# The second expert's list due three f-tiles later, its first rows turned by TensorE, and a search's first counts handed over later

## The chip, the cores and the metric

The kernel runs on one core of a Trainium2 chip. The metric is the device time of one execution in microseconds (us), as the median of several runs. One of the runs of the kernel before was recorded by the hardware profiler; every row below comes from that one execution.

## The reference

An attention without softmax feeds a mixture of experts. The second part is the one that the change touches:

```python
scores = scale * np.matmul(z, z.transpose(0, 2, 1))      # 8 batches of 2496 rows, width 256
attn = np.maximum(scores, 0.0) ** 2
x = (u * np.matmul(attn, v)).reshape(19968, 256)
logits = x @ w_gate                                       # 8 experts
for idx in np.argsort(-logits.flatten()):                 # best pair first, everywhere
    tok, e = idx // 8, idx % 8
    if assigned[tok] >= 0 or counts[e] >= 2496: continue  # an expert takes 2496 rows and is full
    assigned[tok] = e; counts[e] += 1
for e in range(8):
    h = np.maximum(x[assigned == e] @ w1[e], 0.0)         # 256 -> 1024
    out[assigned == e] = h @ w2[e]                        # 1024 -> 256
```

## The kernel before

The attention fills the span up to about 1430 us. The experts follow, one after another, in the order in which they fill up, and the order in which they fill is found while the one before is being computed.

**The work of an expert.** Its 2496 rows are five groups (four of 512 rows, the last of 448). A group takes eight f-tiles, one for each 128 of the 1024 hidden columns. For each f-tile TensorE (PE) computes the first layer into a PSUM tile `hp` (`expand_part`, L672 to L674, three matmuls for each half of the 256 inputs, since every operand is held as a high and a low part). ScalarE (ACT) makes `hh` from it (L750), VectorE (DVE) makes the low part `hl_` (L752; in the group of 448 rows also the tail of `hh`, L755), and three f-tiles later PE does the second layer from both (`contract`, L765, L768, L770) into four accumulators y0 to y3.

**The rows of a group** are fetched by GpSimd (POOL) with four indirect DMAs (`gather_x`, L590), which need the expert's list `idx`. Then they must be turned. Nearly all groups use `tip_x`: DVE transposes blocks of 32 by 32 (L652), SyncE (SP) writes them to DRAM and reads them back in the wanted order (L655, L658), and `split_x` makes the high part on ACT (L665) and the low part on DVE (L666). Only the second group of the first expert uses `turn_x`: eight transposes on PE (L642) into the PSUM tile `xp` and one of the two `hp`, then ACT (L646) and DVE (L647).

Behind a group's last f-tile `put_y` adds the two parts of its rows (L793) and POOL scatters them to the output (L801).

**The route** of expert k (`route(k)`) finds its list, spread over the f-tiles of expert k-1. It closes the expert that is full (L338), finds each row's best open expert (`best_expert`, L80 to L97), and makes sortable integer keys (`order_keys`, L100 to L118). Then it searches a threshold in two stages of six rounds: in a round DVE compares the keys with seven or three candidates (`at_least`, L124, tile `mask`), PE counts the hits (`hist`, L281, tile `srch`), DVE and PE reduce the counts (L286 to L415). From the threshold come the expert's number, the load of its weights and, by a matmul L478 and some matmuls over `ob` (L523, L529), the list `idx` (L534). The weights are split by ACT (L618) and DVE (L621).

**The order.** The main loop writes the program in one fixed order per engine, a step per f-tile: `layer2` of f-tile n, what is due at n, a piece of the route, `layer1` of f-tile n + 3, another piece of the route. The dues are given by `at(n, ...)`: n0 is the first f-tile of a group, and gathers are due at n0 - 12, transposes at n0 - 8, splits at n0 - 4; the second expert's first group (1, 0) has the gather at n0 - 10 and the transpose at n0 - 7. The route's pieces are paced by `advance`: each `yield w` counts w steps, a window of half positions has 88 steps (`YIELDS`), and whatever is left when the window ends is handed over at once. The steps of a route add up to more than 88, so each window ends with such a rest, whose last instructions are the list's; the next route begins right behind it. The windows of the routes 1 and 2 meet at 2 * (PER + LATE), with PER = 40 f-tiles of an expert and LATE = 2.

"Turnover" below is the stretch of a route's end and the next one's start: from the matmul L478 to the first counts L281 of the next route, some 51 us. There are six of them, and a seventh end without a search behind it.

Of the kernel before, what the change touches and what calls it, by code (L numbers as in the profile page):

```python
# [135 lines left out]
def moe(tc, xd, first, jp, identf, w1, w2, out, B, S, cp, dram):  # L136
# [19 lines left out]
    ND = 15  # L156
    LA = 3
    AHEAD = 12
    LATE = 2
    YIELDS = 88  # L160
    with ExitStack() as ctx:
        rp = ctx.enter_context(tc.tile_pool(name="rp", bufs=1))
# [169 lines left out]
        def route(k):  # L332
            if k:
                closed = rp.tile([128, E], F32, name="closed", tag="rab")
                nc.vector.tensor_scalar(closed, ROUTE[k - 1]["star"], SHUT, None, op0=OP.mult)
                for c in range(0, JP, JP // 2):
                    o = lg[:, c:c + JP // 2]
                    nc.vector.tensor_add(o, o, closed[:, None, :].to_broadcast([128, JP // 2, E]))  # L338
                    yield 0.7
                for c in range(0, JP, JP // 4):  # L340
                    eq = rp.tile([128, JP // 4, E], BF, name="eq")
                    best_expert(nc, first, slice(c, c + JP // 4), eq)
                    yield 6.8 / 4
                done = rp.tile([128, JP], F32, name="done")
                with behind(1):
                    nc.vector.tensor_scalar(done, asg, 0.0, GONE, op0=OP.is_gt, op1=OP.mult)
                nc.vector.tensor_add(m, m, done)
                order_keys(nc, first, slice(0, JP))
                yield 1.5
            last = k == E - 1  # L350

            def take():
# [4 lines left out]
            if last:  # L357
                g = rp.tile([128, 2, JP], BF, name="fmask")
                nc.vector.tensor_scalar(g[:, 1], m, -3.1e38, None, op0=OP.is_gt)
                take()  # L360
                full = rp.tile([128, E], F32, name="full")
                nc.vector.tensor_scalar(full, rem, FULL / 2, None, op0=OP.is_lt)
            else:
                with behind(1):
                    nrem = rp.tile([128, E], F32, name="nrem")
                    nc.vector.tensor_mul(nrem, rem, dN)
                    nrow = rp.tile([128, 1], F32, name="nrow")
                    nc.vector.tensor_reduce(nrow, nrem, axis=AX.X, op=OP.add)
                    nc.vector.tensor_copy(hd[:, :, 16], nrow.to_broadcast([128, ND]))
                widths, step, at0, next0 = plans[k > 0]  # L370
                for stage in range(2):
                    V = floor
                    for r, w in enumerate(widths):
                        n = (1 << w) - 1
                        if r == 0:
                            T = first["at0"] if k == stage == 0 else at0
                        else:
                            T = rp.tile([128, ND], I16, name="T", bufs=2)
                            nc.vector.tensor_tensor(T[:, :n], W[:, :n], Dg.to_broadcast([128, n]), op=OP.add)
                        mask = []  # L380
                        whole = first["mask0"] if n > 7 else rp.tile([128, JP, n], BF, name="mask")
                        cuts = [0, JP] if k else [JP - 16, JP] if T is first["at0"] else [0, JP // 2, JP]
                        for lo, hi in zip(cuts, cuts[1:]):
                            at_least(nc, whole, xr, T[:, :n], lo, hi)
                        mask.append((0, lambda j, t=whole, n=n: t[:, j, :n]))
                        yield 2
                        if k:
                            x, nn = hist(mask, n, "jt")
                        else:
                            p, o = quad_hist(mask[0][1], n, r)  # L390
                        warm(k, 4)
                        if r:
                            V2 = rp.tile([128, 1], F32, name="V", bufs=2)
                            nc.vector.tensor_tensor(V2, V, Dg, op=OP.add)
                            V = V2
                        if r == 0:
                            W = next0
                        elif r + 1 < len(widths):
                            W = rp.tile([128, ND], F32, name="W", bufs=2)
                            n2 = (1 << widths[r + 1]) - 1  # L400
                            nc.vector.tensor_tensor(W[:, :n2], step[:, r + 1, :n2], V.to_broadcast([128, n2]), op=OP.add)
                        yield 2.2
                        if k:
                            o = srch()[:, :E * nn]
                            nc.tensor.matmul(o, onesr, x[:, :, :nn], start=True, stop=True)
                        else:
                            quad_sums(p, o, n, "jt")
                        warm(k, 10 if r + 1 < len(widths) or stage else 30)
                        best = rp.tile([128, E, ND], F32, name="best")
                        nc.vector.scalar_tensor_tensor(best[:, :, :n],  # L410
                                                       o.rearrange("p (e t) -> p e t", e=E)[:, :, :n], 0.0,
                                                       step[:, r, None, :n].to_broadcast([128, E, n]),
                                                       op0=OP.is_ge, op1=OP.mult)
                        Dg = rp.tile([128, 1], F32, name="Dg", bufs=2)
                        nc.vector.tensor_reduce(Dg, best[:, :, :n], axis=AX.XY, op=OP.max)  # L415
                    tstar = rp.tile([128, 1], F32, name="tstar")
                    nc.vector.tensor_tensor(tstar, V, Dg, op=OP.add)
                    if stage == 0:
                        base = rp.tile([128, 1], F32, name="base")
                        nc.vector.tensor_scalar(base, tstar, 65536.0, None, op0=OP.mult)  # L420
                        rel = rp.tile([128, JP], F32, name="rel")
                        nc.vector.scalar_tensor_tensor(rel, first["top"], base, first["low"],
                                                       op0=OP.subtract, op1=OP.add)
                        near = rp.tile([128, JP], I16, name="near")
                        nc.vector.tensor_scalar(near, rel, 32767.0, -32768.0, op0=OP.min, op1=OP.max)
                        spread(nc, xr, near)
                        yield 1.5
                T = tstar
                g = rp.tile([128, 2, JP], BF, name="fmask")
                nc.vector.tensor_scalar(g[:, 0], rel, T, None, op0=OP.is_ge)  # L430
                nc.vector.tensor_scalar(g[:, 1], rel, T, None, op0=OP.is_gt)
                take()
                yield
                if k:
                    x, nn = hist([(0, lambda j: g[:, :, j])], 2, "tj")
                    yield
                    o = srch()[:, :E * 2]
                    nc.tensor.matmul(o, onesr, x[:, :, :2], start=True, stop=True)
                else:
                    p, o = quad_hist(lambda j: g[:, :, j], 2, 1)  # L440
                    warm(k, 4)
                    quad_sums(p, o, 2, "tj")
                warm(k, 20)
                o = o.rearrange("p (e t) -> p e t", t=2)
                full = rp.tile([128, E], F32, name="full")
                nc.vector.tensor_scalar(full, o[:, :, 0], 0.0, None, op0=OP.is_ge)
                nc.vector.tensor_scalar(rem, o[:, :, 1], -1.0, None, op0=OP.mult)
# [60 lines left out]
            if k:  # L508
                p = srch()
                for c in range(0, JP, CB):  # L510
# [16 lines left out]
                    for j in range(c, min(J, c + CB)):  # L527
                        n, r = divmod(j - c, QW)
# [283 lines left out]
        def at(n, f, *a):  # L812
            todo.setdefault(n, []).append((f, a))

        for k in range(E):
            for g in range(NG):
                n0 = (k * NG + g) * FT
                if n0:
                    at(1 if (k, g) == (0, 1) else n0 - AHEAD + (LATE if (k, g) == (1, 0) else 0), gather_x, k, g)
                    if (k, g) == (0, 1):  # L820
                        at(n0 - 4, turn_x, k, g, range(DH))
                    else:
                        at(n0 - (7 if (k, g) == (1, 0) else 8), tip_x, k, g)
                        at(n0 - 4, split_x, k, g)
                at(n0 + FT - 1, put_y, k, g)
            n0 = k * PER
# [482 lines left out]
```

## Time and profile before

| what | value |
|---|---|
| median of three runs | 2431.34 us (2430.28 to 2432.57) |
| the profiled execution's own time | 2432.56 us |
| its span | 2430.5 us |
| PE busy | 2380.0 us (98%) |
| DVE busy | 2068.5 us (85%) |
| ACT busy | 1521.4 us (63%) |
| POOL busy | 460.6 us (19%) |

Busy times are sums over the whole span, so an engine with 85% can still be the one that sets the pace in a part of it. The span is shorter than the execution's time by 2.06 us, which lie ahead of and behind the recorded instructions.

### The profile page before, as it was taken

What the parts mean: (1) busy time and instruction counts of PE and PEld (TensorE: products, weight loads), DVE (VectorE), ACT (ScalarE), POOL (GpSimd) and SP (SyncE); (2) the same over time, 40 slices, a digit from 0 to 9 for tenths busy, and PEclk for the clock granted to TensorE, in tenths of its full rate; (3) what the DMA queues carried; (4) which work ended last, traced back from release to release, by engine and by line L of the source; (5) the groups of instructions that cost most, each with busy time, mean ns of one, the idle gap of its engine ahead of it and who ended that gap; (6) DMA issues with size and microseconds to landing.
All of it is one profiled execution on the core that took longest, in us unless ns stands there. A gap on an engine that the chain in (4) does not pass through costs nothing.

```text
span 2430.5 us, 42677 instructions
## 1 busy us (share of the span) xinstructions
PE 2380.0 (98%) x14724; PEld 1983.2 (82%) x14724; DVE 2068.5 (85%) x6220; ACT 1521.4 (63%) x2890; POOL 460.6 (19%) x690
## 2 busy tenths in 40 slices
PE   8999999999999999999999999899999999999998
PEld 6888888888888888888887787787888888888887
DVE  7898998998999998989989798979797979797443
ACT  7888888888888988888888223333332333333332
POOL 3020020020010200200100022333233333333332
PEclk9999999999999999999999999999999999999999
DMA  5153261261251532611511023232323323243331
GB/s 154 43 148 86 57 160 43 58 176 53 71 145 44 138 95 57 159 43 53 137 53 43 10 66 118 78 109 80 115 87 95 111 84 118 78 124 119 98 96 57
DMA packets 233848, 222.28 MB, mean 91 GB/s; under 512 B 95392, under 2 KB 192672, under 8 KB 233504
## 3 DMA queue, kind: packets, MB, share of 16 engines
q1 hardware_dynamic: 193088, 150.58, 21.3%
q0 software_dynamic: 40544, 68.98, 10.5%
q8 instruction: 116, 1.90, 0.3%
q14 instruction: 100, 0.82, 0.1%
HBM read 158.67 MB, written 60.82 MB: 90 GB/s over the span
## 4 chain that ended last, share of the span: by engine, by line
PE 82%; DVE 10%; issue 4%; POOL 1%; ACT 1%; DMA 1%; POOLq 0%; DVEq 0%; SPq 0%; ACTq 0%
PE acc L1038 41%; PE sc L996 11%; PE y L768 8%; PE hp L672 4%; PE hp L674 4%; PE hp L673 4%; PE y L770 4%; PE srch L281 2%; PE acc L1043 1%; POOL xg L590 1%; DVE mask L124 1%; DVE ob L523 1%; DVE w1l L621 1%; PE xp L325 1%; PE srch L529 1%
## 5 line engine op out<-in xcount | busy, mean ns | idle before, releaser
L1025 DVE TENSOR_TENSOR lo<-r,hi 128x512 fp32r<-128x512 f32 (+1 forms) x800 | 536.1, 673 | 83.1 <-ACT hi L1017 80.1
L1038 PE MATMUL acc<-hi,vh 128*128 128x512 f32 (+1 forms) x1520 | 590.8, 389 | 0.2 <-ACT vh L970 0.2
L1038 PE MATMUL acc<-lo,vh 128*128 128x512 f32 (+1 forms) x1520 | 587.7, 387 | 2.7 <-DVE lo L1025 2.7
L1038 PE MATMUL acc<-hi,vl 128*128 128x512 f32 (+1 forms) x1520 | 585.9, 385 | 0.0
L750 ACT ACTIVATE hh<-hp 128x512 fp32r<-128x512 f32 (+1 forms) x319 | 187.3, 587 | 629.9 <-PE hp L674 518.4
L1017 ACT ACTIVATE hi<-r 128x512 fp32r<-128x512 f32 (+1 forms) x780 | 500.2, 641 | 122.1 <-ACT r L1012 87.0
L1012 ACT ACTIVATE r<-r 128x512 f32<-128x512 f32 (+1 forms) x800 | 503.6, 639 | 2.5 <-DVE r L1006 2.4
L1079 DVE SCALAR_TENSOR_TENSOR lt<-xs,wgb 128x256 bf16<-128x256 f32 x1192 | 449.2, 417 | 0.0
L768 PE MATMUL y<-w,hh 128*128 128x512 f32 x1216 | 444.8, 399 | 0.7 <-DVE y L793 0.7
L1038 PEld LDWEIGHTS acc<-hi,vh 128*128 128x128 f32 x1520 | 286.2, 188 | 67.0 <-issue 13.8
L1008 ACT ACTIVATE r<-sc 128x512 f32<-128x512 f32 (+1 forms) x638 | 312.4, 614 | 40.3 <-PE sc L996 39.7
L1038 PEld LDWEIGHTS acc<-lo,vh 128*128 128x128 f32 x1520 | 286.3, 188 | 59.2 <-DVE lo L1025 8.2
L1038 PEld LDWEIGHTS acc<-hi,vl 128*128 128x128 f32 x1520 | 286.3, 188 | 52.1
L590 POOL DMA_INDIRECT xg<-xd,idx x160 | 181.2, 1133 | 513.3 <-DVE xg L628 281.1
L768 PEld LDWEIGHTS y<-w,hh 128*128 128x128 f32 x1216 | 229.0, 189 | 49.0 <-DVE y L793 2.2
L672 PE MATMUL hp<-xh,w1h 128*128 128x512 f32 (+2 forms) x642 | 256.5, 400 | 3.6 <-DVE hh L755 2.7
L673 PE MATMUL hp<-xl,w1h 128*128 128x512 f32 (+2 forms) x642 | 252.5, 393 | 1.2 <-DVE xl L666 1.1
L674 PE MATMUL hp<-xh,w1l 128*128 128x512 f32 (+2 forms) x642 | 250.6, 390 | 0.0
L996 PE MATMUL sc<-z,z 64*128 64x512 f32 (+1 forms) x1920 | 236.9, 389 | 4.2 <-ACT z L961 2.8
L996 PEld LDWEIGHTS sc<-z,z 64*128 64x128 f32 x1920 | 200.7, 185 | 31.2 <-ACT z L961 3.5
L959 POOL DMA_DIRECT2D z<-in_z_dram x35 | 18.7, 534 | 960.0 <-DVE lt L1079 530.0
L801 POOL DMA_INDIRECT out_dram<-y,idx x160 | 160.4, 1003 | 207.8 <-DVE y L793 120.9
(1193 smaller groups left out, 3152.1 us busy)
## 6 DMA issues: line engine op xcount, KB each, us to landing
ur<-in_u_dram SPq DMA_DIRECT2D x39, 512.0 KB
flat<-tr SPq DMA_DIRECT2D x152, 128.0 KB
xt<-flat SPq DMA_DIRECT2D x38, 512.0 KB
vh<-in_v_dram POOLq DMA_DIRECT2D x133, 128.0 KB
vr<-in_v_dram SPq DMA_DIRECT2D x32, 512.0 KB
xd<-tr SPq DMA_DIRECT2D x128, 128.0 KB
xs<-xd SPq DMA_DIRECT2D x32, 512.0 KB
wr<-in_moe_w_dram SPq DMA_DIRECT2D x32, 512.0 KB
```

The lines of the kernel that those rows point to most:

```text
L590: return nc.gpsimd.indirect_dma_start(out=dst, out_offset=None, in_=src, in_offset=bass.IndirectOffsetOnAxis(ap=idx, axis=0))
L672: nc.tensor.matmul(p[:, c], wh, xh, start=(d == 0), stop=False)
L673: nc.tensor.matmul(p[:, c], wh, xl, start=False, stop=False)
L674: latest["mm"] = nc.tensor.matmul(p[:, c], wl, xh, start=False, stop=(d == DH - 1))
L768: nc.tensor.matmul(o, h[:, c], w.rearrange("p s d -> p (s d)"), start=(f == 0), stop=(f == FT - 1), skip_group_check=True)
L996: nc.tensor.matmul(pair[s], key[b, p][r, c * 128:c * 128 + 128], query[b, g][r, :w], start=key is ZH and query is ZH, stop=key is ZL)
L1008: recent["r"] = nc.scalar.activation(r, p, AF.Relu, scale=scale)
L1012: nc.scalar.activation(R[n], R[n], AF.Square)
L1017: nc.scalar.activation(h, R[n], AF.Copy)
L1025: recent["l"] = nc.vector.tensor_sub(LO[n], a, h.bitcast(F32))
L1038: nc.tensor.matmul(o[d], w[:, c[d]], x, start=(kt == 0 and i == 0), stop=False)
L1079: nc.vector.scalar_tensor_tensor(t[r], src[r], 1.0, WG["rows"][r, e], op0=OP.mult, op1=OP.mult, accum_out=lg[r, j, e:e + 1])
```

## The change

It has four edits. `LATE` goes from 2 to 5: the windows of the routes 1 and 2 meet three f-tiles later, and the gather of group (1, 0) is due at n0 - 7. Group (1, 0) is turned by `turn_x` at n0 - 4, in place of `tip_x` at n0 - 7 and `split_x` at n0 - 4. Behind `order_keys` the step counts 3 and not 1.5. In the first round of a search a step of 1 is put between the instructions of the masks and the step of 2 that stands behind every round's masks, so that the counts are handed over later.

```diff
-    LATE = 2
+    LATE = 5
     YIELDS = 88
...
                 order_keys(nc, first, slice(0, JP))
-                yield 1.5
+                yield 3
...
                             at_least(nc, whole, xr, T[:, :n], lo, hi)
+                        if k and r == stage == 0:
+                            yield 1
                         mask.append((0, lambda j, t=whole, n=n: t[:, j, :n]))
                         yield 2
...
                     at(1 if (k, g) == (0, 1) else n0 - AHEAD + (LATE if (k, g) == (1, 0) else 0), gather_x, k, g)
-                    if (k, g) == (0, 1):
+                    if (k, g) in ((0, 1), (1, 0)):
                         at(n0 - 4, turn_x, k, g, range(DH))
                     else:
-                        at(n0 - (7 if (k, g) == (1, 0) else 8), tip_x, k, g)
+                        at(n0 - 8, tip_x, k, g)
                         at(n0 - 4, split_x, k, g)
```

Two lines are added, so that every line behind L385 has a number higher by two in the changed kernel: L281 stays, L672 becomes L674, L752 becomes L754, L768 and L770 become L770 and L772.

The program rows show what moves. First PE at the end of the turnover from route 3 to route 4 (the later ones are alike), before: the second layer of two f-tiles, then the counts.

```order
L768 MATMUL y_24342<-w_22683,hh 128x512
L770 MATMUL y_24342<-w_22683,hl__24329 128x256
L768 MATMUL y_24343<-w_22683,hh 128x512
L770 MATMUL y_24343<-w_22683,hl__24329 128x256
L768 MATMUL y_24344<-w_22683,hh 128x512
L770 MATMUL y_24344<-w_22683,hl__24329 128x256
L765 MATMUL y_24345<-w_22683,hh 128x512
L768 MATMUL y_24342<-w_22683,hh 128x512
L768 MATMUL y_24343<-w_22683,hh 128x512
L768 MATMUL y_24344<-w_22683,hh 128x512
L281 LDWEIGHTS oh
L281 MATMUL srch<-mask,oh 128x112
```

The same place in the changed kernel, the line numbers two higher but for L281:

```order
L770 MATMUL y_24345<-w_22684,hh 128x512
L772 MATMUL y_24343<-w_22684,hl__24374 128x256
L772 MATMUL y_24344<-w_22684,hl__24374 128x256
L674 MATMUL hp<-xh_24191,w1h 128x448
L675 MATMUL hp<-xl_24192,w1h 128x448
L676 MATMUL hp<-xh_24191,w1l 128x448
L674 MATMUL hp<-xh_24195,w1h 128x448
L675 MATMUL hp<-xl_24196,w1h 128x448
L676 MATMUL hp<-xh_24195,w1l 128x448
L772 MATMUL y_24345<-w_22684,hl__24374 128x256
L281 LDWEIGHTS oh
L281 MATMUL srch<-mask,oh 128x112
```

The second-layer matmuls on `hl__24374` and an f-tile's six first-layer matmuls now stand ahead of the counts. On DVE the same place before has the last keys, a piece of the weights' split, the masks, and behind them an f-tile's low part:

```order
L133 COPY rep<-key 128x640
L97 TENSOR_TENSOR oh<-code,code8b 128x320
L116 TENSOR_SCALAR top<-key 128x160
L118 CAST low<-key 128x160
L621 TENSOR_TENSOR w_22683<-wr,w_22683 128x2x256
L366 TENSOR_TENSOR nrem<-rem,dN 128x8
L124 TENSOR_TENSOR mask<-rep,at_17956 128x1120
L368 TENSOR_REDUCE nrow<-nrem 128x1
L752 SCALAR_TENSOR_TENSOR hl__22701<-hp,hh 128x384
```

In the changed kernel it reads:

```order
L133 COPY rep<-key 128x640
L97 TENSOR_TENSOR oh<-code,code8b 128x320
L116 TENSOR_SCALAR top<-key 128x160
L118 CAST low<-key 128x160
L623 TENSOR_TENSOR w_22684<-wr,w_22684 128x2x256
L754 SCALAR_TENSOR_TENSOR hl__22695<-hp,hh 128x384
L757 SCALAR_TENSOR_TENSOR hh<-hp,hh 128x64
L623 TENSOR_TENSOR w_22684<-wr,w_22684 128x2x256
L366 TENSOR_TENSOR nrem<-rem,dN 128x8
L124 TENSOR_TENSOR mask<-rep,at_17956 128x1120
```

An f-tile's low part and one more piece of the split have come between the keys and the masks; the keys still stand ahead of that low part. Last, PE at the first turnover of the changed kernel, where group (1, 0) is turned: the transposes come in pairs, one pair for each of the four gathers, between matmuls of the second layer.

```order
L644 MATMUL xp<-identf,xg 128x128
L644 MATMUL hp<-identf,xg 128x128
L767 MATMUL y_20798<-w_19465,hh 128x512
L644 MATMUL xp<-identf,xg 128x128
L644 MATMUL hp<-identf,xg 128x128
L770 MATMUL y_20795<-w_19465,hh 128x512
L644 MATMUL xp<-identf,xg 128x128
L644 MATMUL hp<-identf,xg 128x128
L770 MATMUL y_20796<-w_19465,hh 128x512
L770 MATMUL y_20797<-w_19465,hh 128x512
```

On DVE, where the list (`idx`, 18 instructions earlier) is made by the rest of route 1, the low parts of these rows stand among the instructions of `best_expert` of route 2:

```order
L80 TENSOR_REDUCE m<-lg 128x40
L95 TENSOR_TENSOR code<-eq 128x40
L80 TENSOR_REDUCE m<-lg 128x40
L97 TENSOR_TENSOR oh<-code,code8b 128x320
L82 TENSOR_TENSOR eq<-lg,m 128x320
L754 SCALAR_TENSOR_TENSOR hl__21056<-hp,hh 128x384
L84 TENSOR_TENSOR eq<-eq,code8b 128x320
L757 SCALAR_TENSOR_TENSOR hh<-hp,hh 128x64
L91 TENSOR_TENSOR eq<-eq 128x40x4
L649 TENSOR_TENSOR xl_21078<-xp,xh_21077 128x512
L93 TENSOR_TENSOR eq<-eq 128x40x2
L649 TENSOR_TENSOR xl_21082<-hp,xh_21081 128x512
```

Both L649 come 18 and 20 instructions behind the list, and the rest of the keys and the masks of route 2 stand behind them.

## Rows read from the trace of the kernel before

**Rows 1.** PE's waits by cause, 1540 to 2431: total us, times, longest.

```profile
PE srch L281 <- DVE mask L124: 9.8, 5, 3.3
```

**Rows 2.** Timeline of PE: start, us, instruction, idle before it and releaser.

```profile
1562.42 0.66 PE L281 MATMUL srch<-mask,oh 128*128 128x112 bf16 x10 [0.51 <-PE y L765]
...
1564.54 0.50 PE L673 MATMUL hp<-xl,w1h 128*128 128x512 f32 x1 [0.87 <-DVE xl L666]
...
1680.20 0.35 PE L281 MATMUL srch<-mask,oh 128*128 128x112 bf16 x2 [3.32 <-DVE mask L124]
...
2185.38 0.38 PE L770 MATMUL y<-w,hl__29448 128*128 128x256 f32 x1 [2.04 <-DVE hl__29448 L752]
```

**Rows 3.** Stretches: us, busy PE, PEld, DVE, ACT, POOL, PEclk, DMA, GB/s.

```profile
1509.05:1556.65 47.60, 42.17 (x336) 35.92 (x335) 47.39 (x116) 16.62 (x28) 12.69 (x12) 0.93 0.34 112
1547.28:1549.35 2.07, 2.07 (x12) 1.79 (x12) 2.07 (x8) 0.00 (x0) 1.46 (x3) 1.00 0.24 87
...
1629.22:1680.20 50.98, 47.66 (x377) 40.25 (x377) 50.08 (x117) 19.70 (x35) 18.51 (x16) 1.00 0.38 123
1680.20:1755.73 75.53, 75.52 (x471) 62.29 (x471) 58.81 (x190) 22.81 (x45) 24.26 (x24) 0.98 0.29 84
1755.73:1806.93 51.20, 49.08 (x383) 41.62 (x382) 50.58 (x118) 19.66 (x35) 19.34 (x16) 1.00 0.40 124
1806.93:1881.35 74.42, 74.29 (x471) 60.98 (x471) 58.72 (x190) 22.81 (x45) 24.29 (x24) 1.00 0.29 85
...
1680.20:1683.40 3.20, 3.20 (x18) 3.03 (x18) 3.20 (x11) 0.00 (x0) 0.00 (x0) 0.50 0.50 160
...
2058.25:2061.45 3.20, 3.20 (x19) 2.94 (x19) 3.20 (x11) 0.00 (x0) 0.00 (x0) 0.59 0.50 162
```

**Rows 4.** Timeline of DVE, the masks of route 4, then two rows of other places.

```profile
1805.40 0.67 DVE L621 TENSOR_TENSOR w<-wr,w 128x512 fp32r<-128x512 f32 x1
1806.00 0.15 DVE L366 TENSOR_TENSOR nrem<-rem,dN 128x8 f32<-128x8 f32 x1
1806.08 0.80 DVE L124 TENSOR_TENSOR mask<-rep,at 128x1120 bf16<-128x1120 int16 x1
...
1806.88 0.54 DVE L752 SCALAR_TENSOR_TENSOR hl__24380<-hp,hh 128x384 fp32r<-128x384 f32 x1
...
1442.57 0.68 DVE L752 SCALAR_TENSOR_TENSOR hl__19574<-hp,hh 128x512 fp32r<-128x512 f32 x1
...
1543.06 1.09 DVE L621 TENSOR_TENSOR w1l<-wr,w1h 128x512 fp32r<-128x512 f32 x1
```

**Rows 5.** Timeline of PE, matmuls back to back.

```profile
1801.30 0.28 PE L770 MATMUL y<-w,hl__24282 128*128 128x256 f32 x1
1801.42 0.39 PE L765 MATMUL y<-w,hh 128*128 128x512 f32 x1
1801.65 0.36 PE L672 MATMUL hp<-xh,w1h 128*128 128x448 f32 x1
1801.85 0.36 PE L673 MATMUL hp<-xl,w1h 128*128 128x448 f32 x1
```

**Rows 6.** Timelines of POOL and DVE: the gather and turning of group (1, 0).

```profile
1540.50 0.99 POOL L590 DMA_INDIRECT xg<-xd,idx  x1 [25.84 <-DVE idx L534]
...
1545.23 0.95 POOL L590 DMA_INDIRECT xg<-xd,idx  x1 [0.30 <-issue]
...
1549.58 1.24 DVE L652 STREAM_TRANSPOSE tr<-xg 128x1024 f32<-128x1024 f32 x1
```

**Rows 7.** Timelines of POOL, PE and ACT: group (0, 1), turned by PE.

```profile
1440.76 1.00 POOL L590 DMA_INDIRECT xg<-xd,idx  x1 [0.30 <-issue]
...
1443.66 0.33 PE L642 MATMUL xp<-identf,xg 128*128 128x128 f32 x1 [0.39 <-DMA xg<-xd,idx]
1443.83 0.60 PE L642 MATMUL hp<-identf,xg 128*128 128x128 f32 x4
...
1444.03 0.60 ACT L646 ACTIVATE xh<-xp 128x512 fp32r<-128x512 f32 x1 [1.86 <-PE xp L642]
```

## The prediction

> **What bounds the kernel now.** I read the table of busy times first, then PE's waits by cause, then the timeline at each wait, and last the stretches around them. PE is busy for 98% of the span, so there are few microseconds to win, and all of them in the experts' part lie where PE waits. The list of causes names one above all: five times the first counts of a search, L281, wait for DVE's masks, 9.8 us together, 3.3 us at most [rows 1]. The timeline shows the longest at 1680.20 and a wait of another kind, 2.04 us at the seventh turnover, where the second layer waits for DVE's low part [rows 2]. The reader is to see next, in the stretches, that a turnover is DVE's time and the rest of a period PE's: from 1755.73 to 1806.93 DVE is busy 50.58 of 51.20 us and PE 49.08, from 1806.93 to 1881.35 PE is busy 74.29 of 74.42 us and DVE 58.72 [rows 3]. The turnovers at 1509 and 1629 look alike: DVE 47.39 of 47.60 and 50.08 of 50.98 us [rows 3]. Two rules follow. In a turnover an instruction more on DVE makes the turnover longer by its whole time. And PE work that is moved from the turnover into the rest of the period costs its whole time too, since PE has no room there, while in the turnover it lay in PE's waits.
>
> **The later counts at the four last turnovers.** These are from route 3 on to the end of route 6. I counted in the program order what stands between L478 and the first counts (at the last one, the same stretch), before and now. PE has six matmuls of 448 columns more, seven of 512 columns in the first layer less, four of 512 in the second layer less (one for each of y0 to y3) and one of 256 less. Start to start they take 0.20, 0.23 and 0.12 us [rows 5], so 1.20 - 1.61 - 0.92 - 0.12 = -1.45 us of PE work. DVE has one L621 of the second weights more, 0.60 us from its start to the next one's [rows 4], and one low part of 512 columns is replaced by one of 384 and a short tail, which I set equal (0.68 against 0.54 us and the tail [rows 4]). So the turnover is longer by 0.60 us and holds 1.45 us less of PE's work: 2.05 us lost, PE's wait there growing from 51.20 - 49.08 = 2.12 [rows 3] to about 4.2 us. Four times this is 8.2 us. The masks are hidden by the f-tile that now stands ahead of the counts. What is late next is that f-tile's neighbour: the low part `hl__24374`, which the second layer needs, stands on DVE behind the keys and an L621, so the wait changes its name from L281 to L772. Behind the waiting L772 PE's queue holds the next six matmuls of the first layer, and the counts. If DVE has 0.60 us of slack that I don't see, a turnover costs 1.45; if the tail and the L621 run at their full 0.67 with a tail of some 0.1 to 0.2, it costs 2.3. I keep 5.8 to 9.2 for the four and take 8.2.
>
> **The later counts at the turnover from route 2 to route 3.** The same count gives six matmuls of 448 more, seven of 512 in the first layer less, eight of 512 and five of 256 in the second layer less: 1.20 - 1.61 - 1.84 - 0.60 = -2.85 us of PE work. DVE has one L621 more and one low part of 512 less, 0.60 against 0.68: nothing. I take +2.85, with 1.5 as the low end, if the pieces missing there include some that PE would have done in a wait anyway.
>
> **The second expert's first rows.** At the first turnover DVE gets two L621 of the first weights (1.09 each [rows 4]), one of the second (0.60), two L647 (no row of the size is shown; the nearest is the 128x512 of 0.68 [rows 4]) and loses two L652 of 1.24 [rows 6]; of the low parts two of 512 go and three of 384 come, 3 * 0.54 - 2 * 0.68 = 0.26. Sum: 2.18 + 0.60 + 1.36 - 2.48 + 0.26 = 1.9, and with the three tails 2.0. SP loses five DMAs, which nothing else waits for. On POOL the gather moves behind the scatters of group (0, 3); so far these stood behind it while POOL was idle for the list [rows 6], and only the buffer of y hangs on them, so I take nothing for it. The transposes add some 0.95 us to PE: eight, of which four are done in 0.60 us, 0.15 each at most [rows 7].
>
> Then there is a wait that was not there. The rows are fetched once the list is there: POOL stood 25.84 us idle for it [rows 6]. A gather takes 0.99 us and 0.30 to the next, so the fourth starts 3.87 after the first; in this place it was 4.73, since the third took longer [rows 6]. A gather lands 2.90 us after its start (1440.76 to 1443.66), ACT starts 0.37 later and takes 0.60 [rows 7]. So L647 can't start until 3.87 + 2.90 + 0.37 + 0.60 = 7.7 us (8.6 by the slower gathers) after the first gather. Between the list and L647 DVE has 18 short instructions; in a stretch of such ones eight take 2.07 us, seven of them whole [rows 3], so 18 take 4.7 to 5.3. DVE, which had been busy throughout, stands for 2.4 to 3.9 us at L647; I take 2.6, near the quicker gathers, as the longer one was a single case. Queued behind it are the rest of the keys and the masks of route 2, and for these PE's counts wait. PE itself also waits for the gathers at the pairs of transposes, which falls into the same time. The turnover gets 2.0 + 2.6 = 4.6 us longer and loses, by the same count, some 0.8 us of PE's old work (six of 448 more, and 512-column ones less). That is 5.4 us, from which the two waits behind it go, 0.51 and 0.87 [rows 2], the latter the wait for the low part of just these rows. 4.0 us remain. Were the gathers quick and the DVE work hidden, it would be 1; were they as slow as before, 5.3.
>
> On this the Trainium skill, VectorE: DVE Perf Modes, section "Rules for kernel authors", speaks for the change: a full 128 x 128 transpose belongs on TensorE where the result may go to PSUM. The trace agrees as far as DVE goes, 1.24 us of L652 against 0.95 of PE [rows 6, 7]; that the rows would then be turned for nothing lost is rival D.
>
> **PE's clock.** Behind the wait of 3.32 us the granted clock was 0.50 for 3.2 us (that is 1.2 GHz against 2.4), and 0.59 at 2058.25, behind the same wait at another turnover [rows 3]; over the stretch that begins at 1806.93 it stayed 1.00 [rows 3]. The rest of a period with such a spell took 75.53 us, without one 74.42: 1.1 us [rows 3]. So before, two of the five steady turnovers paid 1.1 each. Now each of the five has a wait in which most of 4.2 us lies, and the nearest row, 3.32, fell. I count four falls of five against two, 2.2 us, and take 2.0. No fall at all would give -2.2, a fall behind each of six waits +4.4.
>
> The Trainium skill, TensorE: Matmul & The Clock Gate, section "Why this matters for your kernels", advises against idle gaps of a few microseconds between bursts of matmuls, as these bring the low clock back; the trace agrees at 3.32 us. By that rule all five turnovers fall, and the sum would be 1.1 us higher.
>
> **Sum.** 8.2 + 2.85 + 4.0 + 2.0 = 17.05 us. The profiled execution took 2432.56 us, its span 2430.5 with 2.06 outside it; so 2449.6 us for an execution like it. The median of the runs shown is 1.22 us lower, which makes 2448.4 us. The terms' own ends give 5.8 + 1.5 + 1 - 2.2 = 6.1 and 9.2 + 2.85 + 5.3 + 4.4 = 21.8 us; they are not all low or all high together, so the likeliest case's own range is 2440 to 2453 us.
>
> **The rivals.**
> A, faster: the f-tile between masks and counts covers the masks, and no wait takes their place. Then the 9.8 us of L281 [rows 1] and the 2.04 us of the seventh end [rows 2] go and nothing comes: 2431.3 - 11.8 = 2419.5 us. For it: the counts are the chief cause of waiting. Against: DVE has no idle time in a turnover, so its masks' time must come out of some wait. It decides at one point: whether the low part of the f-tile, in DVE's queue behind the keys, is done before PE gets to its L772. By my count it is more than 3 us late.
> B, no change: the stretch that I count is only cut elsewhere. If PE has room in the rest of a period, the 1.45 us aren't lost, and DVE's 0.60 lies beside them; the turnovers then cost 4 * 0.6, the first one its 4.0, and the clock gives its 2.2 back, since the waits are split among several instructions: 2431.3 + 2.4 + 4.0 - 2.2 = 2435.5 us. Against it: 74.29 of 74.42 us [rows 3].
> C, slower still: the gathers at the turn take 8.6 us and more, and with DVE's long stand at L647 and the six waits PE's clock falls at each: 8.2 + 2.85 + 5.3 + 4.4 = 20.8, 2452 us, and up to 2456 if PE's first layer then also runs into the half clock in the turnover itself.
> D, slower, but less: the rows are there in time, DVE is rid of L652 and doesn't stand at L647; then the 2.6 us go, and of the other 2.8 half stays hidden by the waits that the turnover has anyway, 5.43 us of PE by the first stretch [rows 3]. The first turnover costs nothing: 2444.4 us.
>
> **How the numbers follow.** My forecast has a chance of 0.52, D 0.13, C 0.14, B 0.13, A 0.08. A run of this kernel can tell a change from none at about 0.2%, here 4.9 us: below 2426.5 is faster, above 2436.2 slower. So faster is 0.08, the same 0.13, slower 0.79. The range reaches from 2436, the upper edge of B, to 2455, most of C; it leaves out A, most of B and the end of C.
>
> **What would show it right or wrong.** In the profile after, PE's waits should name L772 <- L754 (five or so times, over 3 us each) in place of L281 <- L124, and the period between two turnovers should be 2 us longer than 125.62 (51.20 + 74.42). At the first turnover DVE should stand 2 to 4 us at L649 for ACT, and PE at L644 for the gathers. The clock row should show a spell of 0.5 behind most of the turnovers. I am wrong if the waits for the masks are simply gone and the period is 125 us or less, if DVE shows idle time in the turnovers from route 3 on, or if the rest of a period still takes 74.4 us while the turnover has not grown.

## The result, and the profile after

The changed kernel takes 2452.08 us (median of 4, 2450.02 to 2455.52) against 2430.81 us before: 21.3 us more, a ratio of 1.0084 [1.0070, 1.0098]. It was predicted slower, at 2448.4 us with a range of 2436 to 2455. The profiled execution took 2453.21 us.

PE's waits by cause in the experts' part of the changed kernel come first (total us, times, longest); line numbers behind L385 are two higher than before.

```profile
PE srch L531 <- DVE ob L525: 5.1, 8, 3.1
PE srch L281 <- DVE mask L124: 3.2, 2, 3.0
PE y L772 <- DVE hl__24374 L754: 3.2, 1, 3.2
PE y L772 <- DVE hl__26053 L754: 3.2, 1, 3.2
PE y L772 <- DVE hl__27732 L754: 3.2, 1, 3.2
PE y L772 <- DVE hl__29411 L754: 3.2, 1, 3.2
PE y L772 <- DVE hl__22695 L754: 3.2, 1, 3.2
...
PE srch L281 <- DVE fmask L433: 1.5, 4, 0.4
```

Of the 9.8 us of waits for the masks [rows 1] 3.2 are left, 3.0 of them at the first turnover, and five waits of 3.2 us at the second layer have come, as forecast. The largest row was not forecast: at L531, the matmuls over `ob` that make a list, PE waits 5.1 us, 3.14 of them at 1544.81 in the first turnover. Before, that wait was 1.91 us, at 1537.07, just ahead of the window of [rows 1]. What stands on DVE ahead of such a wait is seen in its timeline at the turnover from route 4 to route 5; PE's wait ends at 1944.71.

```profile
1943.21 0.23 DVE L116 TENSOR_SCALAR top<-key 128x160 f32<-128x160 int16 x1
1943.36 0.23 DVE L118 CAST low<-key 128x160 f32<-128x160 int16 x1
1943.51 0.68 DVE L623 TENSOR_TENSOR w<-wr,w 128x512 fp32r<-128x512 f32 x1
1944.11 0.54 DVE L754 SCALAR_TENSOR_TENSOR hl__26053<-hp,hh 128x384 fp32r<-128x384 f32 x1
...
1945.39 0.81 DVE L124 TENSOR_TENSOR mask<-rep,at 128x1120 bf16<-128x1120 int16 x1
```

The low part is made as soon as the keys and a piece of the weights are done, with no idle time between; the masks come behind it and keep nobody waiting. The stretches of the same turnovers and of the rest of their periods (us, busy PE, PEld, DVE, ACT, POOL, PEclk, DMA, GB/s) answer to [rows 3]; the cut between the two lies here at the end of PE's wait at L772, not at the counts, which come 2 to 3 us later:

```profile
1762.68:1813.65 50.97, 46.60 (x367) 38.96 (x367) 49.02 (x117) 19.08 (x34) 17.69 (x16) 0.99 0.38 123
1813.65:1894.05 80.40, 79.86 (x487) 65.73 (x488) 60.66 (x192) 23.53 (x46) 25.09 (x24) 0.96 0.27 79
1894.05:1944.71 50.66, 46.69 (x366) 38.93 (x367) 49.11 (x115) 19.19 (x34) 16.58 (x16) 1.00 0.39 125
1944.71:2024.10 79.39, 78.70 (x487) 64.66 (x488) 60.56 (x192) 23.41 (x46) 25.41 (x24) 0.98 0.27 80
1684.92:1688.12 3.20, 3.19 (x24) 2.93 (x25) 3.03 (x11) 1.04 (x2) 0.00 (x0) 1.00 0.45 152
1813.00:1819.00 6.00, 5.35 (x23) 4.70 (x24) 3.98 (x16) 1.10 (x3) 0.00 (x0) 0.50 0.37 111
1946.00:1949.00 3.00, 3.00 (x18) 2.52 (x17) 2.02 (x10) 1.08 (x2) 0.00 (x0) 0.50 0.52 175
```

The second of these periods is 50.66 + 79.39 = 130.05 us long, where 51.20 + 74.42 = 125.62 was the measure before [rows 3]. Of the 4.4 us more, PE was not busy for 4.66 in place of 2.25 us, so 2.4 are waiting: 1.3 because the wait of the turnover is 3.23 and not 1.95 us, and 1.1 in smaller waits, none over 0.4. PE was busy for 125.39 in place of 123.37, so 2.0 are the same work done more slowly; from 1946 the granted clock was 0.50. In the period before it the low clock lasted from 1813 to 1819, and the period is 131.37 us. Behind the wait that ends at 1684.92 the clock stayed at 1.00, though that wait was as long. Between 1440 us and the last f-tiles the clock fell at six places (1546, 1567, 1812, 1946, 2075, 2205), before at three (1540, 1680, 2058).

The rows of the second expert, in the order POOL, PE, DVE:

```profile
1547.80 0.99 POOL L592 DMA_INDIRECT xg<-xd,idx  x1 [11.60 <-DVE idx L536]
...
1551.64 0.95 POOL L592 DMA_INDIRECT xg<-xd,idx  x1 [0.30 <-issue]
...
1553.26 0.33 PE L644 MATMUL xp<-identf,xg 128*128 128x128 f32 x1 [0.67 <-DMA xg<-xd,idx]
...
1555.46 0.69 DVE L649 TENSOR_TENSOR xl<-xp,xh 128x512 fp32r<-128x512 f32 x1 [2.78 <-ACT xh L648]
...
1566.66 0.21 PE L281 MATMUL srch<-mask,oh 128*128 128x112 bf16 x1 [3.02 <-DVE mask L124]
```

The gathers start 3.84 us apart, first to fourth, DVE stands 2.78 us at L649 (2.6 were forecast), and PE's first counts of route 2 wait 3.02 us for the masks behind it, where they waited 0.78 before.

Where the time was lost along the span is read from the start of the same f-tile's low part (L752, now L754) in both timelines:

| f-tile, counted from the first after 1440 us | before | after | difference | lost since the row above |
|---|---|---|---|---|
| first | 1442.57 | 1440.54 | -2.03 | |
| 49th, behind the first turnover | 1607.96 | 1608.17 | 0.21 | 2.2 |
| 93rd, behind 2 to 3 | 1748.90 | 1751.91 | 3.01 | 2.8 |
| 133rd, behind 3 to 4 | 1874.51 | 1883.25 | 8.74 | 5.7 |
| 173rd, behind 4 to 5 | 2000.21 | 2013.35 | 13.14 | 4.4 |
| 213th, behind 5 to 6 | 2127.22 | 2143.56 | 16.34 | 3.2 |
| 253rd, behind 6 to 7 | 2251.51 | 2272.47 | 20.96 | 4.6 |

From there on the difference stays at 21.0. The 2.03 us at the start lie in the attention, which is the same program in both; that is how two executions differ.

### The profile page after: what moved, and what is told of

Its sections match the earlier page's. It is cut to its first block, busy times and chain, and to the rows that moved or that the text cites. A ratio compares the mean times of both kernels' runs of the same rounds, so it can differ in the third digit from the quotient of the medians.

```text
span 2451.4 us, 42668 instructions
## 1 busy us (share of the span) xinstructions
PE 2388.2 (97%) x14732; PEld 1986.9 (81%) x14732; DVE 2068.4 (84%) x6219; ACT 1522.3 (62%) x2890; POOL 455.1 (19%) x690
## 4 chain that ended last, share of the span: by engine, by line
PE 78%; DVE 13%; issue 5%; POOL 2%; ACT 1%; DMA 1%; another core or an unknown queue 0%; DVEq 0%; POOLq 0%; SPq 0%; ACTq 0%
PE acc L1040 41%; PE sc L998 11%; PE y L770 7%; PE hp L674 4%; PE hp L675 4%; PE y L772 4%; PE hp L676 4%; DVE ob L525 2%; PE srch L281 1%; PE acc L1045 1%; POOL xg L592 1%; DVE hl L519 1%; DVE w1l L623 1%; PE xp L325 1%; POOL out_dram L803 1%
## 5 line engine op out<-in xcount | busy, mean ns | idle before, releaser
L752 ACT ACTIVATE hh<-hp 128x512 fp32r<-128x512 f32 (+1 forms) x319 | 187.3, 587 | 654.2 <-PE hp L676 440.7
L770 PE MATMUL y<-w,hh 128*128 128x512 f32 x1216 | 444.7, 400 | 0.3 <-DVE y L795 0.3
L592 POOL DMA_INDIRECT xg<-xd,idx x160 | 174.9, 1093 | 510.9 <-DVE xg L630 208.1
L770 PEld LDWEIGHTS y<-w,hh 128*128 128x128 f32 x1216 | 228.5, 188 | 47.7 <-DVE y L795 0.7
L674 PE MATMUL hp<-xh,w1h 128*128 128x512 f32 (+2 forms) x642 | 257.3, 401 | 4.4 <-DVE hh L757 2.9
```

Of the source, the lines that this page charges most:

```text
L592: return nc.gpsimd.indirect_dma_start(out=dst, out_offset=None, in_=src, in_offset=bass.IndirectOffsetOnAxis(ap=idx, axis=0))
L674: nc.tensor.matmul(p[:, c], wh, xh, start=(d == 0), stop=False)
L770: nc.tensor.matmul(o, h[:, c], w.rearrange("p s d -> p (s d)"), start=(f == 0), stop=(f == FT - 1), skip_group_check=True)
```

## Experiments

Ratios are against the kernel before, run on the same chip; where a time of it isn't given again, it is the last one named.

**The parts alone.** Three kernels with one part each and one with both steps.

```diff
 late_turn:  LATE = 5; group (1, 0) by turn_x; steps as before
 y3:         behind order_keys
-                yield 1.5
+                yield 3
 y1:         behind the first round's masks
+                        if k and r == stage == 0:
+                            yield 1
 y3y1:       both steps, LATE = 2, tip_x
```

Expected of late_turn: 

> LATE = 5 and turn_x for group (1, 0) alone; both yields as before. Theory (the turnovers are DVE's time, and the two yields push PE's work out of them): 2 to 4 us slower than before (2433 to 2435), all of it up to the first counts of route 2; from route 3 on the periods between two L478 are 125.6 to 126 us as before, PE waiting 1.9 to 2 us at L281 for the masks. Rival (the later list and its shorter window for route 2 are what costs): over 10 us slower, most of the whole change's 21.

Measured: 2436.07 against 2432.34 us, 1.0010 [1.0000, 1.0019]. At the edge of what can be told, and near the upper end of the theory; the rival falls. Its later waits are those of before, as PE's row at the turnover 3 to 4 shows:

```profile
1810.18 0.21 PE L281 MATMUL srch<-mask,oh 128*128 128x112 bf16 x1 [1.91 <-DVE mask L124]
```

Expected of y3: 

> The step behind the keys counts 3, LATE = 2, no step between the first masks and counts. Theory: by the program order the wait turns already here from L281 to L770 on the low part behind the keys, and each turnover from route 2 on gets some 1.4 us longer, five times, with some 1.5 more for PE's clock where it falls: 8 to 15 us slower (2439 to 2446). Rival (the later list costs most): 0 to 4.

Measured: 2447.83 us, 1.0063 [1.0047, 1.0080], 15.5 us. The wait has the new name and size already, and the clock fell behind all five of them. The time is just above the 8 to 15 us that were expected.

```profile
1941.49 0.58 PE L770 MATMUL y<-w,hl__26052 128*128 128x256 f32 x1 [3.04 <-DVE hl__26052 L752]
```

Expected of y1: 

> A step of 1 between the first masks and their counts, LATE = 2, 1.5 behind the keys as before. Theory: PE's wait stays at L281 for the masks, since the masks stand where they stood, and grows from 1.9 to about 2.9 us, because a piece of the route that was handed over ahead of the window's end now belongs to the rest and lies in the turnover: 5 to 12 us slower (2436 to 2443). Rival (a step between masks and counts gives DVE room, so the wait shrinks): 2 to 8 us faster.

Measured: 2440.77 us, 1.0032 [1.0021, 1.0043], 8.4 us. PE still waits at L281, longer, as the theory had it:

```profile
1936.76 0.21 PE L281 MATMUL srch<-mask,oh 128*128 128x112 bf16 x1 [2.65 <-DVE mask L124]
```

Expected of y3y1: 

> Both steps, LATE = 2 and tip_x as before: the change without the second expert's part. Theory: 13 to 19 us slower (2444 to 2450), less than y3 and y1 add up to, the profile from route 3 on like that of the whole change, PE waiting over 3 us at L770 for the low part. Rival: under 10 us, with the second expert's part making the rest of 21.

Measured: 2456.33 us, 1.0095 [1.0077, 1.0114], 24.0 us: slower than expected, as much as the two parts add up to (23.9), and not less than the whole change (21.3), though the intervals overlap. So the steps are what costs, and beside them the second expert's part costs little or nothing at this pace.

**PE's clock.** The whole change with idle work in the place of waiting.

```diff
+  in contract, before L770 of y0, for f-tile 3 of group 4 of the experts 1 to 5:
+                for _ in range(26):      # into the free tile xp, read by nobody, in this order
+                    nc.tensor.matmul(z[:, :256], tri, slot..., start=True, stop=True)
```

Expected: 

> The whole change, and in each of the five waits of 3.2 us at the low part (expert 1 to 5, group 4, f-tile 3) 26 matmuls of 256 bf16 columns into the free xp tile, whose result nobody reads: some 3 us of PE work in the place of waiting. Theory (much of what the prediction missed is PE's clock, which falls behind these waits; in the profile of the change 17 us at 0.50 behind four of them): the spells from 1700 us on are gone and it takes 7 to 9 us less than the change, 2443 to 2446 (ratio to before about 1.005). Rival (DVE sets the pace there, so the clock costs little): 2450 to 2453 as the change.

Measured: 2439.08 against 2429.81 us, 1.0040 [1.0026, 1.0054], so 9.3 us over before and 12 less than the change's 21.3 (11 by the two ratios), more than the 7 to 9 that were expected. The waits of 3.2 us became 0.35 (L779 is the second layer's matmul on the low part in this kernel), and behind them the clock stays up:

```profile
1936.73 0.50 PE L779 MATMUL y<-w,hl__26107 128*128 128x256 f32 x2 [0.35 <-DVE hl__26107 L752]
```

```profile
1937.50:1940.50 3.00, 3.00 (x24) 2.72 (x23) 2.85 (x11) 1.64 (x3) 0.00 (x0) 1.00 0.48 174
```

The periods are 127.2 to 127.35 us, 1.6 to 1.7 over before. But for the added matmuls the instructions of PE, DVE, ACT and POOL stand in the same order as in the changed kernel, so the same matmul can be looked up in both profiles, once at the end of each wait and once where the change is back at the full clock:

| turnover | end of the wait: change, with idle work | at the full clock again: change, with idle work | lost between the two |
|---|---|---|---|
| 2 to 3, clock at 1.00 throughout | 1684.92, 1682.41 | 1689.80, 1687.29 | 0.0 |
| 3 to 4 | 1813.65, 1809.59 | 1819.69, 1812.89 | 2.7 |
| 4 to 5 | 1944.71, 1936.73 | 1949.56, 1940.01 | 1.6 |
| 5 to 6 | 2075.03, 2064.03 | 2079.29, 2066.72 | 1.6 |
| 6 to 7 | 2205.34, 2191.41 | 2209.04, 2193.55 | 1.6 |

Four spells of the low clock thus cost 7.4 us. From the matmul L478 (L480 in the change) of the second turnover, at 1634.69 against 1633.26, to that of the seventh end, at 2210.42 against 2195.01, the change loses 14.0 us, so the clock is about half of what the idle work gives back. The other half lies in smaller waits, at L531 for `ob` and at L281 for `fmask` among others, which the kernel with idle work hardly has. They are not the clock's: from 1634.69 to 1762.68 the change ran at 1.00, and still this period took 128.00 us against 126.31. One source is seen on ACT behind the turnover, where the change (first row) makes `hh` 1.5 us later than the kernel with idle work (second row):

```profile
1777.99 0.60 ACT L752 ACTIVATE hh<-hp 128x512 fp32r<-128x512 f32 x1 [3.68 <-remote]
```

```profile
1773.34 0.60 ACT L750 ACTIVATE hh<-hp 128x512 fp32r<-128x512 f32 x1 [2.13 <-PE hp L674]
```

The profile doesn't name what ACT waited for in the change, and why the added matmuls take this away is open.

**Is a turnover DVE's time?** Two kernels write a round's masks three times, one in the turnover and one in the rest of the period; a third does a reduction of the keys twice.

```diff
 dve_turn (routes 2 to 6; dve_rest: r == stage == 1, the second round of the second stage)
-                        for lo, hi in zip(cuts, cuts[1:]):
+                        for lo, hi in list(zip(cuts, cuts[1:])) * (3 if k > 1 and r == stage == 0 else 1):
 keys_twice, ahead of best_expert
+                    if k > 1: nc.vector.tensor_reduce(m[:, c:c + JP // 4], lg[:, c:c + JP // 4], axis=AX.X, op=OP.max)
```

Expected of dve_turn: 

> The kernel before, with the first round's masks of the routes 2 to 6 written three times (the same values): two more L124 of 0.73 us between the keys and the first counts, in five turnovers. Theory (a turnover is DVE's time): each turnover gets 1.5 us longer, 7.3 in all, and 0 to 5 more for PE's clock, since the waits grow to over 3 us: 2438 to 2444. Rival (PE's work sets the period, a DVE instruction costs only if it is in PE's way at the moment): under 2435.

Measured: 2430.91 us, 1.0003 [0.9993, 1.0013]: no change, against the theory. DVE's timeline shows why:

```profile
1806.22 0.82 DVE L124 TENSOR_TENSOR mask<-rep,at 128x1120 bf16<-128x1120 int16 x1
...
1807.02 0.55 DVE L752 SCALAR_TENSOR_TENSOR hl__24386<-hp,hh 128x384 fp32r<-128x384 f32 x1
...
1807.56 0.82 DVE L124 TENSOR_TENSOR mask<-rep,at 128x1120 bf16<-128x1120 int16 x1
...
1808.43 0.81 DVE L124 TENSOR_TENSOR mask<-rep,at 128x1120 bf16<-128x1120 int16 x1
```

The scheduler put the added masks behind the low part `hl__24386`, for which PE was waiting (until 1807.62, 2.44 us), and PE's work on it covers them. So the rule in the prediction was too wide: not every instruction of the turnover costs its whole time. That only those cost which stand ahead of the first thing that PE waits for is argued from this, not shown, since PE's order changed too: the counts moved behind that f-tile's second layer, from 1806.93 to 1810.20.

Expected of dve_rest: 

> The kernel before, with the masks of the first round of the second stage of the routes 2 to 6 or of their second round written three times: as many instructions more as in the kernel with the first masks three times, but in the rest of the period, where DVE is busy 58.7 of 74.4 us. Theory: no change, 2430 to 2434. Rival (DVE as a whole is near its limit): 2437 to 2442 as with the masks of the turnover.

Measured: 2429.66 us, 0.9998 [0.9988, 1.0007]; as expected, but after dve_turn it tells the two places no longer apart.

Expected of keys_twice: 

> The kernel before, with the first reduction of the keys (L80, a row's best open expert, 0.39 us from start to start) done twice for each of the four quarters in the routes 2 to 7: 1.6 us more on DVE, this time well ahead of the last keys and of everything that PE waits for at a turnover (the second masks turned out to lie behind it). Theory, as mended (only DVE's work ahead of the first thing that PE waits for costs, and that costs its whole time): PE's waits at L281 grow from 1.9 to some 3.4 us, 1.4 to 1.6 us in each of six turnovers, 8 to 10 us, and 3 to 7 more for PE's clock, which falls behind waits of this length: 2441 to 2447. Rival (the turnover is not DVE's time, as the second masks suggested): 2429 to 2434.

Measured: 2450.65 against 2434.69 us, 1.0067 [1.0050, 1.0083], 16 us, within the 11 to 17 that the two terms of its theory add up to: the mended rule holds. Two turnovers of it, PE's waits and the stretches:

```profile
1946.12 0.26 PE L281 MATMUL srch<-mask,oh 128*128 128x112 bf16 x2 [3.25 <-DVE mask L124]
...
2073.70 0.26 PE L281 MATMUL srch<-mask,oh 128*128 128x112 bf16 x2 [3.22 <-DVE mask L124]
```

```profile
1893.33:1946.12 52.79, 49.36 (x382) 41.58 (x382) 52.27 (x123) 19.54 (x35) 17.75 (x16) 1.00 0.35 112
1946.12:2021.08 74.96, 74.54 (x471) 60.88 (x471) 58.77 (x190) 22.73 (x45) 23.99 (x24) 1.00 0.31 90
2021.08:2073.70 52.62, 49.19 (x383) 41.56 (x382) 52.16 (x122) 19.54 (x35) 19.20 (x16) 1.00 0.34 113
2073.70:2151.58 77.88, 75.87 (x471) 62.29 (x471) 58.92 (x190) 22.74 (x45) 24.49 (x24) 0.98 0.29 86
```

The turnovers are 1.4 to 1.6 us longer than the 51.20 of before, the DVE work that was added. The rest of the period is 74.96 us where the clock stayed up and 77.88 where it fell, 2.9 us more. These are not all the clock's: PE is busy 1.33 us longer with the same work, and 1.6 us are waiting that comes later in the period. The six turnovers are not alike either, as the first period grew by 4.6 us (124.74 against 120.17), which was not traced further.

**The pace.** Routes spread over the whole window, so that no rest is handed over at its end.

```diff
-    YIELDS = 88
+    YIELDS = 106        # pace106: with the whole change; pace106_before: with nothing else;
+                        # steps_pace106: with both steps, LATE = 2, tip_x
+    ... * ({1: 100, 2: 100}.get(k, 110))   # pace_by_route: steps and LATE of before, turn_x
```

Expected of pace106: 

> The whole change with YIELDS = 106, so that a window holds all of a route's steps (their sum is 105.5) and no rest is handed over at its end. Theory (the steps cost only because they push as much of the route into the rest, which lies in the turnover): PE's waits behind the keys shrink from 3.2 to about 1 us or less, no half clock there, the periods go down to 124 us: 2410 to 2420, faster than before. Rival (the second list or the later counts cost by themselves): 2445 or more.

Measured: 2415.42 against 2429.81 us, 0.9940 [0.9923, 0.9956]: the same change is 14.4 us faster than before when the pace goes with it. PE no longer waits in a turnover, though DVE is as busy there as ever, and the clock stays at 1.00 from 1500 to 2400 us. The counts come later here, at 1920.44, and PE is busy up to them:

```profile
1862.20:1914.00 51.80, 51.80 (x397) 43.91 (x398) 50.85 (x111) 19.17 (x38) 19.83 (x16) 1.00 0.38 122
1914.00:1986.39 72.39, 71.61 (x456) 58.16 (x455) 59.20 (x197) 23.12 (x44) 25.26 (x24) 1.00 0.30 88
```

Expected of pace106_before: 

> The kernel before with YIELDS = 106 and nothing else. Theory (the rest of a route that is handed over at a window's end is what makes the turnover DVE's time): 8 to 14 us faster than before, 2416 to 2422, and 2 to 6 us behind the whole change with the same pace, 2415. Rival (the change's own steps and turned rows make that kernel's gain): 2428 or more.

Measured: 2438.12 against 2434.69 us, 1.0015 [1.0005, 1.0024]. The theory fails: without the steps the pace alone gains nothing. The waits went elsewhere, to 1.42 us and more in each period at the first layer, and 3.77 at the last route's end:

```profile
2003.92 0.50 PE L672 MATMUL hp<-xh,w1h 128*128 128x512 f32 x1 [1.42 <-DVE hl__27024 L752]
...
2200.81 0.50 PE L672 MATMUL hp<-xh,w1h 128*128 128x512 f32 x1 [3.77 <-ACT xh L665]
```

Expected of pace_by_route: 

> The steps and LATE of before, group (1, 0) turned by PE, and a pace for each route: 100 for the routes 1 and 2, 110 for the others. Theory: no rest is left, as at 106 with the change; 2412 to 2418, the best or as good as the whole change at 106. Rival (without the later keys and counts the masks are waited for again): over 2420.

Measured: 2436.11 us, 1.0012 [1.0002, 1.0021]. The rival: its periods are 128.1 us, and in each four waits of 0.7 to 1.05 us are spread over it.

Expected of steps_pace106: 

> Both steps with YIELDS = 106, but LATE = 2 and group (1, 0) by tip_x as before. Before alone at 106 was no faster than at 88, the whole change at 106 was 14 us faster. Theory (what is won there is that the later keys and counts stand between f-tiles, with a window that holds all 105.5 steps; the second expert's part is worth a few us): periods from route 3 on of 124.1 to 124.4 us as with the whole change, 2415 to 2421. Rival (the second expert's part makes the gain): 2428 or more.

Measured: 2428.86 against 2432.77 us, 0.9983 [0.9973, 0.9992]: between the two. So at this pace the steps gain 7 to 8 us (against pace106_before) and the second expert's part some 10 more. Part of that is one wait behind the seventh end, with a fall of the clock, which the whole change doesn't have:

```profile
2194.04 0.50 PE L672 MATMUL hp<-xh,w1h 128*128 128x512 f32 x1 [2.85 <-DVE hl__29637 L752]
```

Three steady periods, 125.2 against 124.2 us, make 3 us more, though PE, DVE and ACT do the same in the same order there; why is open. Another 3.7 us are lost ahead of them, by the matmul L478 of the third turnover (1741.78 against 1738.07).

## Why the prediction was right, step by step

- **The wait changes its name** (likeliest case): shown. Five waits of 3.2 us at L772 for the low part behind the keys, the masks hidden, and y3 shows that the step behind the keys alone does it. Rival A fell at the point that was named: the low part was 3.2 us late.
- **The four last turnovers, 8.2 us**: near in size, in part by luck. The waiting grew by 2.4 us per period against 2.05 forecast, but the wait that was named only grew from 1.95 to 3.23 us, not from 2.12 to 4.2; the other 1.1 us are smaller waits that the count didn't hold. A period costs 1.6 to 1.7 us with idle work in the wait, and some 3 in the change itself with its low-clock spell taken off.
- **The rule behind it** (an instruction more on DVE in a turnover costs its whole time): too wide. Ahead of the first thing that PE waits for it cost its time, 1.4 to 1.6 us for 1.6 in keys_twice; two masks behind it cost nothing that could be measured in dve_turn, where PE's order changed too. In the forecast the counted L621 stood on the right side.
- **Route 2 to 3, 2.85 us**: 2.8 lost in the table, but in part by luck, since the fall of the clock that the kernel before had at 1680 is missing there, worth 1.1 us [rows 3]; without this the term would have been about one too small.
- **The second expert's rows, 4.0 us**: the stand at L649 was 2.78 us as forecast, but only 2.2 us are lost behind the first turnover in the profile; late_turn alone lost 3.7, at the edge of what can be told. The term left out a wait of before that went with the old order (second row below). It also left out that four of the eight adds of `put_y` in this turnover, 1.40 us of DVE (first row), now stand outside it. Both rows are of the kernel before:

```profile
1509.06 1.40 DVE L793 TENSOR_TENSOR y<-y,y 128x256 f32<-128x256 f32 x4
...
1540.90 0.71 PE L672 MATMUL hp<-xh,w1h 128*128 128x448 f32 x1 [2.74 <-DVE hh L755]
```

- **The transposes, 0.95 us of PE**: this doesn't follow from its row, since eight at up to 0.15 us are up to 1.2. No term of the sum used it.
- **The clock, 2.0 us**: mis-sized by 2 to 3 us. The count was about right (four falls in five waits, one twice as long), the price was not: 1.1 us was read from two periods of different turnovers, and matched matmul by matmul a spell costs 1.6 us and the long one 2.7, so 7.4 for the four. The two spells of before (1680 and 2058), at 1.1 by [rows 3] or 1.6 by the table, come off, which leaves 4 to 5 us against 2.0. Rival C had 4.4 here, from more falls at the smaller price. The wait at 2058.25 was also misread as the same as the one of 3.32 us. It was 1.90 us long, and behind one of the same length the clock stayed up, as PE's rows and the stretches behind them show in the kernel before:

```profile
1932.57 0.65 PE L281 MATMUL srch<-mask,oh 128*128 128x112 bf16 x10 [1.90 <-DVE mask L124]
...
2058.25 0.65 PE L281 MATMUL srch<-mask,oh 128*128 128x112 bf16 x10 [1.90 <-DVE mask L124]
```

```profile
1932.57:1935.77 3.20, 3.20 (x25) 2.96 (x25) 3.20 (x11) 0.73 (x2) 0.00 (x0) 1.00 0.46 163
2058.25:2061.45 3.20, 3.20 (x19) 2.94 (x19) 3.20 (x11) 0.00 (x0) 0.00 (x0) 0.59 0.50 162
```

- **The sum**: the time was 3.7 us above the forecast. In the two profiled executions 23.0 us are lost from the first f-tile of the table on, against 17.05 forecast: the first turnover was taken 1.8 too high, and the other terms together came out some 8 higher than forecast. The changed execution was 2.0 us ahead at that f-tile, which hides part of this. That it is slower, and by which wait, was reasoned rightly; that the total came so near is luck in part.

By the clock rule of the Trainium skill, TensorE: Matmul & The Clock Gate, section "Why this matters for your kernels", all five waits would have had a fall behind them; the trace agrees at four and at one (1684.92) it doesn't.

## What to carry to other kernels

Where two engines take turns at setting the pace, look on the slower one at what stands ahead of the first thing that the other waits for, and move that forward: there 1.6 us of work cost 1.4 to 1.6 us per turnover. A pause of PE can have two prices, the pause and the slow matmuls behind it; here the pause grew by 1.3 us and the slow matmuls took 1.6 or more. Idle work put into a pause can change more than the clock, so compare the two profiles matmul by matmul before the whole gain is put down to it. A pacing constant has to be tried together with the steps that it paces: the same change cost 21 us with the old constant and gained 14 with another, which by itself gained nothing.

## What the runs showed of the hardware

In the changed kernel a wait of 3.2 us left the granted clock at 1.00 once (1684.92) and brought 0.50 four times in the same execution, and once the low clock lasted over 6 us (1813 to 1819). In the kernel before a wait of 1.90 us had a fall behind it at 2058.25 and none at 1932.57. A spell at 0.50 behind such a wait of 3.2 us cost 1.6 us, and the long one 2.7.
